# A gated recurrence, sixteen expert blocks and a gated FFN on one core: shorter lead in the first rounds, the first tokens as whole rows, gathers spread out, the last weights split earlier

## The chip, the core and the metric

The kernel runs as one program on one core of a Trainium2 chip. It uses the core's five engines: TensorE (PE), VectorE (DVE), ScalarE (ACT), GpSimd (POOL) and SyncE (SP, which here only starts transfers), and 16 DMA engines. The metric is the device time of one execution in microseconds (us). Three executions of the kernel before took 1109.24, 1110.06 and 1112.05 us; the median is 1110.06 us.

## The reference

Three steps follow one another, all in fp32. The first is a gated linear recurrence for 4 batches x 8 heads with a head size of 48, over 768 positions:

```
f = sigmoid(f_logit)
for t in range(768):
    state = f[t][:, None] * state + k[t] outer v[t]
    y[t]  = q[t] @ state
x = y.transpose(0, 2, 1, 3).reshape(3072, 384)
```

The second is a mixture of 8 experts (384 to 1024 to 384). Each of the 3072 tokens goes to the two experts with the largest noisy logits:

```
logits = x @ w_gate + log1p(exp(x @ w_noise)) * noise
w      = softmax of the two largest logits
out[token] = sum over its two experts e of  w_e * (relu(x[token] @ w1[e]) @ w2[e])
```

The third is `out = (silu(xn @ w_gate) * (xn @ w_val)) @ w_out` with `xn` the rms-normed tokens (times `rms_g`) and a middle size of 1536.

## The kernel before

**Fp32 products.** A large product is done as three products of operands that are split into a rounded high part and the rest (`three`, L650 to L656): high x high, high x low, low x high. A weight is split when a *part* of it is taken from its loaded tile (`Part.finish`, L192 to L209): an expert's part takes an ACT copy for `whi` (L208) and a DVE subtraction for `wlo` (L209). A part of the FFN comes as pairs of words of a 64-bit input, so it first goes through `narrow` (L177 to L181: one ACT and three DVE instructions for each of its 2 or 3 pieces), then the ACT copy (L204), and the subtraction runs on POOL (L205). Split parts lie in 18 slots, 8 of pool `wp` and 10 of pool `wp2`.

**Stage 1, the recurrence** (`gla_stream`). The sequence is cut into 24 chunks of 128 positions. Round i of the loop computes chunk i on PE: `scores` (L391), `keys` of the next chunk (four transposes, L172), `rows` of the previous chunk (the router's logits and the tokens, L453), `inter` (L431), `state` (L406) and `attend` (L441). What a chunk needs first is made in steps by ACT and DVE: `clip` (L327, L329), `gates` (L336, L337), `sums` (a scan, L343) and `prep` (exponentials L363 and L368, products KT L365 and QT L370). Round i runs `prep` for chunk i+2, `sums` for i+3, `gates` for i+4 and `clip` for i+5, so the first chunks of all of these must be ready before round 1 is through. `warm` puts filler matmuls (L1015) between the first rounds; there are 29. `columns` and `yT` are the operands of `rows`, `AM` the masked scores, `Ss` the running state.

**The router** (`router`) takes the logits of the first 1536 tokens, chooses their experts and makes lists of token numbers, `stoka` (L622). Its steps are put between the rounds by `plan`, a table of round numbers, at most three steps to a round (`safe`). One of its products, `bank<-r_both` (L514, L516), counts the tokens that go to each expert; it stands on PE behind `scores` of round 15.

**Gathers.** An expert block's tokens come by indirect transfers issued by POOL (L730): one instruction brings 128 pieces of 96 numbers (384 B), and a block of 384 tokens takes 12 of them. For the first block they stand in rounds 20 to 24 of `plan`, three to a round. Gathers of later blocks are given to units of the expert stage, two at most to a unit (`room`), except that those of block 1 pile up at unit 0, since there is no earlier unit: in the code that is `at_unit = max(at_unit, 0)`. `paced` makes a gather wait for the ACT instruction in `mark`, which is set by the expert stage. The gathered tokens `xg` are turned by a DVE transpose to `xt`, and split by ACT and DVE into `xhi` (L643) and `xlo` (L644). For block 0 this stands behind the recurrence.

**Stage 2, the experts and the FFN** (`expert_stream`). There are 128 units for the experts (16 blocks x 8 units: the first 8 blocks take early tokens from `stoka`, the other 8 the rest) and 72 for the FFN (6 blocks x 12). A unit is a first product (`l1`), an activation (`hhi` by ACT, `hlo` by DVE: L758 and L759 for experts, `sg`, L852 and L853 for the FFN) and a second product, two units later. After each unit `take_part` may split one part of the weights to come, in the order of the list `parts`. The FFN's 18 parts stand at the list's end; after one is taken, none is taken in the next two units (`count["rest"] = g_ + 2`).

PE follows the written order through both stages. In stage 1 so do ACT, DVE and POOL; in stage 2 a scheduler orders these.

Of the kernel before, what the change touches and what calls it, by code (L numbers as in the profile page):

```python
# [9 lines left out]
F32 = mybir.dt.float32  # L10
# [17 lines left out]
def tile_gated_attention_moe_ffn(  # L28
# [107 lines left out]
    stoka = cp.tile([P, 4, E, CAPA // P], I32, name="stoka")  # L136
    sel = ep.tile([P, 4, 4, 32], F16, name="sel")
# [126 lines left out]


# [47 lines left out]
    def load_v(n):  # L313
        b, c = divmod(n, NCH)
        nc.sync.dma_start(Vs[n % NV][:, :DM], v[b, c * P:(c + 1) * P])

# [58 lines left out]
    def keys(n):  # L375

        if n % NCH == NCH - 1:
            return
        p = cut(bank("K"), HP, P)
        for a in range(HP):  # L380
            flip(p[:, a, :], st["KT", n][:, a, :], ident)
        nc.scalar.activation(Ks[n % NK][:, :, :D],
                             p.rearrange("p a (b d) -> p (a b) d", b=2)[:, :, :D], AF.Copy)

    def scores(n):
        QT = st["QT", n]
        KT = st["KT", n]
        p = pa.tile([P, 2, HP, P], F32, name="scores")
        for h in range(H):
            o = 64 * (h % 2)  # L390
            nc.tensor.matmul(p[:, h % 2, h // 2, :], KT[o:o + D, h // 2, :],  # L391
                             QT[o:o + D, h // 2, :], start=True, stop=True)
        t = st["AM", n] = wk.tile([P, H, P], F32, name="AM", bufs=1)
# [41 lines left out]
    def attend(n):  # L435
        c = n % NCH
        pY = st["pY", n]
        for a in range(HP):
            for g in range(2):
                h = 2 * a + g  # L440
                nc.tensor.matmul(pY[64 * g:64 * (g + 1), a, :], Vs[n % NV][:, h * D:h * D + 64],  # L441
                                 st["AM", n][:, g * HP + a, :], start=not c and a == 0,
                                 stop=a == HP - 1, skip_group_check=True)
        y = wk.tile([P, HP, P], F32, name="yT", bufs=1)
        with tc.high_priority(30):
            nc.scalar.activation(y, pY, AF.Copy)
        st["yT", n] = y
# [57 lines left out]
    def router(n0, n1, rp):  # L505
# [59 lines left out]
        else:  # L565
# [3 lines left out]
                        float(-MIDDLE), op0=OP.min, op1=OP.max)  # L569
        yield  # L570
# [103 lines left out]
    late = {}  # L674
    mark = [None, None]
# [26 lines left out]
    def x_tiles(b, n):  # L702
        b.xhi = late["x"].tile([P, KD, 512], F32R, name="xhi")
        b.xlo = late["x"].tile([P, KD, 512], F32R, name="xlo")

    def h_tiles(n):
        return [xs_.tile([P, 512], F32R, name=nm, bufs=3) for nm in ("hhi", "hlo")]

    def moe_block(e, t0, N, pid):
# [12 lines left out]
        table = (xd[:NTA * P] if t0 == 0 else xd).rearrange("n (g d) -> (n g) d", g=4)  # L722

# [24 lines left out]
        b.turns = [lambda i=i: turn(i) for i in range(len(rows))]  # L748

# [19 lines left out]
        def post():  # L769
            for i, r in enumerate(rows):  # L770
                y = xs_.tile([P, DM], F32, name="y", bufs=3)
# [17 lines left out]
    def ffn_block(bi):  # L789
# [76 lines left out]
        def post(which=range(4)):  # L866
            for i in which:
                n = 4 * bi + i
                y = xs_.tile([P, DM], F32, name="y", bufs=3)
# [40 lines left out]
    free = [(wp, str(i), -1) for i in range(8)]  # L910
# [9 lines left out]
    def take_part(g_):  # L920
# [16 lines left out]
        if part.wide and units[g_][0] < NM:  # L937
            count["rest"] = g_ + 2
# [15 lines left out]


    wanted = []
    for i in range(1, len(blocks)):
# [63 lines left out]
    def gla_stream():  # L1021
# [3 lines left out]
        with tc.manual_schedule(engines=ALL):  # L1025
# [13 lines left out]
            nc.sync.dma_start(columns[:, :, NX:], moe_w_both[:, :, :2 * E])  # L1039
            for t in Vs:  # L1040
# [4 lines left out]
            run(prep, 0, PARTS)  # L1045
            warm(3)
            keys(0)
            next(rest)
            run(decay, 1)
            next(rest)  # L1050

            for i in range(NT + 2):
                routing.extend(plan.get(i, []))
                n = 4 + 2 * i if i < 2 else i + 6
                if (i < 2 or i % 2 == 0) and valid(n):
                    load_kq(n)
                if valid(i + 3):
                    load_v(i + 3)
                n = 6 + 2 * i if i < 2 else i + 8
                if (i < 2 or i % 2 == 0) and valid(n):  # L1060
                    load_f(n)
# [3 lines left out]
                if i == 0:  # L1065
                    warm(6)
                    run(prep, 1)
                more = prep(i + AHEAD) if i and valid(i + AHEAD) else iter(())
                next(more, None)
                if valid(i + 1):  # L1070
# [3 lines left out]
                if valid(i - 1):  # L1074
                    rows(i - 1)
                if valid(i):
                    inter(i)
                safe()
                next(more, None)
                if i == 0:  # L1080
                    warm(4)
                if valid(i):
                    state(i)
                    carry(i)
                    if i == 0:
                        attend(i)
                if i == 0:
                    warm(6)
                    run(decay, 2)
                    clip(3, scalar=False)  # L1090
                    gates(3)
                    run(prep, 2)
                    clip(4, scalar=False)
                if valid(i + 4):
                    gates(i + 4)
                if valid(i) and i:
# [30 lines left out]
    late["x"] = main.enter_context(tc.tile_pool(name="xl", bufs=2))  # L1127
    wp2 = main.enter_context(tc.tile_pool(name="wp2", bufs=1))
    late["cv"] = main.enter_context(tc.tile_pool(name="cv", bufs=2))
    free.extend((wp2, str(i), -1) for i in range(10))  # L1130
    for fn in blocks[0].turns:
        fn()
# [256 lines left out]
```

## Time and profile before

| | |
|---|---|
| Median of three executions | 1110.06 us |
| Profiled execution: its own time | 1109.45 us |
| Profiled execution: span | 1107.7 us |
| PE busy | 1049.3 us (95%) |
| DVE busy | 665.5 us (60%) |
| ACT busy | 484.6 us (44%) |
| POOL busy | 307.1 us (28%) |
| Recurrence: first `scores` to first expert matmul | 7.9 to 166.46 us |
| Experts: to first activation of the FFN | to 621.4 us |
| FFN: to the last matmul | to 1098.7 us |

The span runs from the first to the last instruction in the trace; the execution's own time holds 1.75 us more. In the rows below "PEclk" is the clock that PE was granted, as a share of 2.4 GHz. A time in square brackets at the end of a timeline row is how long the engine stood idle before it, and what it waited for; "issue" means that the profile shows nothing it waited for, "remote" that it waited for a semaphore whose setter the profile does not name.

### The profile page before, as it was taken

Reading aid. Unit: us, or ns where it says so; the run is one execution under the profiler, and the core shown is the slowest. Engines: PE = TensorE matmul, PEld = TensorE weight load, DVE = VectorE, ACT = ScalarE, POOL = GpSimd, SP = SyncE. Lnnn points to the kernel's source line nnn. Section 1 sums busy time; section 2 is a strip of 40 time slices with the busy share of each in tenths; the row PEclk is TensorE's granted clock in tenths of the full one; section 3 lists DMA queues with packets and bytes.
Section 4 is the critical chain, followed back from the end, with each engine's and each line's share of the span. In section 5 each row is a group of like instructions: output and inputs, shape, how many; then the busy total and the mean of one; then the engine's idle time right before and its main releaser. Section 6 shows DMA issues by size and latency. Waiting matters only on the chain.

```text
span 1107.7 us, 17452 instructions
## 1 busy us (share of the span) xinstructions
PE 1049.3 (95%) x6497; PEld 950.0 (86%) x6497; DVE 665.5 (60%) x1475; ACT 484.6 (44%) x1048; POOL 307.1 (28%) x327
## 2 busy tenths in 40 slices
PE   6998858999999999999999987899999999999996
PEld 4887748999999999899999976788888888888886
DVE  5889946977666656655555689545344454454332
ACT  5886624556555544454443545323223223232211
POOL 2000224544455544444441163220030020110000
PEclk8999977999999999999999998899999999999999
DMA  9976232667666655455443263020020110110000
GB/s 304 321 232 207 64 98 84 218 222 232 216 214 212 199 172 167 145 157 161 136 154 95 92 200 114 29 73 15 1 86 1 44 43 1 57 30 1 29 1 32
DMA packets 89138, 134.46 MB, mean 121 GB/s; under 512 B 8847, under 2 KB 65059, under 8 KB 89043
## 3 DMA queue, kind: packets, MB, share of 16 engines
q1 hardware_dynamic: 79475, 113.82, 31.3%
q0 software_dynamic: 9568, 19.43, 6.6%
q8 instruction: 53, 0.87, 0.3%
q14 instruction: 42, 0.34, 0.1%
HBM read 107.63 MB, written 25.59 MB: 120 GB/s over the span
## 4 chain that ended last, share of the span: by engine, by line
PE 76%; DVE 9%; issue 6%; DMA 4%; ACT 2%; POOL 1%; SPq 1%; POOLq 0%; DVEq 0%; ACTq 0%
PE bank L656 68%; DMA raw<-in_moe_w_dram 3%; PE bank L441 2%; PE scores L391 1%; PE bank L453 1%; PE bank L431 1%; PE bank L172 1%; DVE wlo L209 1%; PE bank L406 1%; DVE cv L179 1%; DVE AM L395 1%; DVE cv L181 1%; POOL wlo L205 1%; DVE cs L343 1%; DVE KT L365 1%
## 5 line engine op out<-in xcount | busy, mean ns | idle before, releaser
L656 PE MATMUL bank<-xhi,wlo 128*128 128x512 f32 (+8 forms) x816 | 305.0, 374 | 11.7 <-POOL wlo L205 10.6
L656 PE MATMUL bank<-xhi,whi 128*128 128x512 f32 (+8 forms) x816 | 305.7, 375 | 6.6 <-ACT xhi L643 4.7
L656 PE MATMUL bank<-xlo,whi 128*128 128x512 f32 (+8 forms) x816 | 304.0, 373 | 0.0
L656 PE MATMUL bank<-whi,hhi 128*128 128x384 f32 x728 | 245.6, 337 | 2.3 <-ACT y L775 0.9
L656 PE MATMUL bank<-whi,hlo 128*128 128x384 f32 x728 | 245.7, 337 | 0.9 <-issue 0.9
L656 PE MATMUL bank<-wlo,hhi 128*128 128x384 f32 x728 | 245.3, 337 | 0.4 <-issue 0.4
L656 PEld LDWEIGHTS bank<-xhi,wlo 128*128 128x128 f32 x816 | 155.5, 191 | 31.4 <-POOL wlo L205 11.9
L656 PEld LDWEIGHTS bank<-xhi,whi 128*128 128x128 f32 x816 | 155.4, 190 | 28.1 <-ACT xhi L643 4.9
L656 PEld LDWEIGHTS bank<-xlo,whi 128*128 128x128 f32 x816 | 155.3, 190 | 16.8 <-DVE xlo L644 0.3
L209 DVE TENSOR_TENSOR wlo<-raw,whi 128x256 fp32r<-128x256 f32 (+1 forms) x320 | 137.7, 468 | 31.9 <-ACT whi L208 26.3
L759 DVE SCALAR_TENSOR_TENSOR hlo<-bank,hhi 128x384 fp32r<-128x384 f32 (+7 forms) x128 | 73.2, 572 | 117.5 <-ACT hhi L758 106.9
L208 ACT ACTIVATE whi<-raw 128x256 fp32r<-128x256 f32 (+1 forms) x320 | 126.3, 451 | 32.2 <-DMA raw<-in_moe_w_dram 28.9
L656 PEld LDWEIGHTS bank<-whi,hhi 128*128 128x128 f32 x728 | 133.7, 184 | 7.6 <-DVE y L773 1.5
L656 PEld LDWEIGHTS bank<-wlo,hhi 128*128 128x128 f32 x728 | 133.3, 183 | 7.7 <-issue 1.0
L656 PEld LDWEIGHTS bank<-whi,hlo 128*128 128x128 f32 x728 | 133.3, 183 | 4.6 <-issue 1.2
L730 POOL DMA_INDIRECT xg<-xd,stokr x107 | 105.0, 981 | 106.3 <-ACT hhi L758 82.1
L730 POOL DMA_INDIRECT xg<-xd,stoka x96 | 100.4, 1045 | 112.7 <-ACT hhi L758 77.0
L758 ACT ACTIVATE hhi<-bank 128x384 fp32r<-128x384 f32 (+7 forms) x128 | 64.1, 501 | 152.2 <-PE bank L656 126.9
L849 DVE TENSOR_TENSOR sg<-bank,sg 128x512 f32<-128x512 f32 x72 | 49.7, 690 | 118.1 <-ACT sg L848 118.0
L800 POOL DMA_INDIRECT xg<-yd,slots x40 | 44.2, 1104 | 237.4 <-ACT hhi L852 207.4
L848 ACT ACTIVATE sg<-bank 128x512 f32<-128x512 f32 x72 | 42.9, 596 | 142.8 <-PE bank L656 136.3
L852 ACT ACTIVATE hhi<-sg 128x512 fp32r<-128x512 f32 x72 | 45.4, 630 | 116.9 <-DVE sg L850 116.7
(161 smaller groups left out, 1057.0 us busy)
## 6 DMA issues: line engine op xcount, KB each, us to landing
raw<-in_moe_w_dram SPq DMA_DIRECT2D x64, 768.0 KB
Qs<-in_kq_dram SPq DMA_DIRECT2D x11, 1024.0 KB
yd<-y SPq DMA_DIRECT2D x48, 192.0 KB
Fs<-in_f_logit_dram SPq DMA_DIRECT2D x11, 512.0 KB
Vs<-in_v_dram SPq DMA_DIRECT2D x24, 192.0 KB
xd<-x SPq DMA_DIRECT2D x24, 192.0 KB
ya<-y SPq DMA_DIRECT2D x24, 192.0 KB
raw<-in_moe_w_gate_dram SPq DMA_DIRECT2D x6, 768.0 KB
```

Of the source, the lines that this page charges most:

```text
L172: nc.tensor.transpose(p, x, i)
L208: nc.scalar.activation(hi[:, j], raw[:, j], AF.Copy)
L209: nc.vector.tensor_tensor(lo[:, j], raw[:, j], hi[:, j].bitcast(F32), op=OP.subtract)
L441: nc.tensor.matmul(pY[64 * g:64 * (g + 1), a, :], Vs[n % NV][:, h * D:h * D + 64], st["AM", n][:, g * HP + a, :], start=not c and a == 0, ...
L656: nc.tensor.matmul(o, a, b, start=start and i == 0, stop=stop and i == 2)
L730: paced(nc.gpsimd.indirect_dma_start(out=b.xg[i][:, k_], out_offset=None, in_=table, in_offset=bass.IndirectOffsetOnAxis(ap=rows_of[:, k_, ...
L758: mark[0] = nc.scalar.activation(hhi[:, :N], p[:, :N], AF.Relu).ins
L759: mark[1] = nc.vector.scalar_tensor_tensor(hlo[:, :N], p[:, :N], 0.0, hhi[:, :N].bitcast(F32), op0=OP.max, op1=OP.subtract).ins
L800: paced(nc.gpsimd.indirect_dma_start(out=y, out_offset=None, in_=ya if n < GROUP else yd, in_offset=bass.IndirectOffsetOnAxis(ap=at_, axis ...
L848: nc.scalar.activation(sg, ps[0], AF.Sigmoid)
L849: nc.vector.tensor_tensor(sg, ps[0], sg, op=OP.mult)
L852: mark[0] = nc.scalar.activation(hhi, sg, AF.Copy).ins
```

## The change

It has four parts.

1. In the first rounds each chunk is prepared one round later: round i does `prep` for i+1, `sums` for i+2, `gates` for i+3 and `clip` for i+4. In rounds 2, 3, 4 and 5 `clip`, `gates`, `sums` and `prep` in turn do two chunks (`due`), and from round 6 the lead is that of before. `keys` and `scores` are split from what follows them (`keys_out`, `masks`) in the prologue, `keys` stands behind `inter` while i is below 6, and 20 fillers are left of 29.
2. The first block's tokens come as 3 gathers of 128 whole rows (1536 B; `fetch_rows`) with the list `stok0`, in rounds 19 and 20. They are turned by 9 PE transposes in rounds 22 and 23 and split from PSUM (`turn_rows`). `xhi` and `xlo` move to the pool `xs_`, `hhi`, `hlo` and `y` to a late pool.
3. Eight of block 1's 12 gathers are issued in rounds 20 to 24, about two to a round, and paced by `yT`, which now sets `mark`. The router runs one step earlier.
4. Of the FFN's 18 loads of weights, 12 are put among the last 48 loads of the experts, one after every fourth. Slots are 6 of `wp` and 12 of `wp2`; the wait between the FFN's parts is one unit.

```diff
-    free = [(wp, str(i), -1) for i in range(8)]
+    EARLY = 24
+    experts = loads[:]
+    del loads[:], parts[:]
+    ...
+    ffn = loads[:]
+    loads[:] = experts[:-2 * EARLY]
+    for i, load in enumerate(experts[-2 * EARLY:]):
+        loads.append(load)
+        if i % 4 == 3 and wide:
+            loads.append(ffn.pop(0))
+    loads += ffn
+    parts[:] = [part for load in loads for part in load.parts]
+    free = [(wp, str(i), -1) for i in range(6)]
...
-            count["rest"] = g_ + 2
+            count["rest"] = g_ + 1
...
+        def fetch_rows(i):
+            b.xg[i] = xs_.tile([P, 4, DM // 4], F32, name="xg", bufs=6)
+            paced(nc.gpsimd.indirect_dma_start(
+                out=b.xg[i].rearrange("p b d -> p (b d)"), out_offset=None, in_=xd[:NTA * P],
+                in_offset=bass.IndirectOffsetOnAxis(ap=stok0[:, i:i + 1], axis=0)))
+        def turn_rows(i):
+            if i == 0:
+                x_tiles(b, N)
+            p = cut(bank("X"), KD, P)
+            x = b.xg[i].rearrange("p b (c k) -> p k (b c)", k=KD)
+            for j in range(KD):
+                flip(p[:, j], x[:, j], ident)
+            c = slice(i * P, (i + 1) * P)
+            split_x(b.xhi[:, :, c], b.xlo[:, :, c], p)
...
+        skip = GIVEN if i == 1 else 0
         for u, fns in zip(where, b.fetches):
+            fns, skip = fns[skip:], max(0, skip - len(fns))
...
+            def due(i, grows, lead):
+                if i < grows:
+                    ns = (i + lead,)
+                elif i == grows:
+                    ns = (i + lead, i + lead + 1)
+                else:
+                    ns = (i + lead + 1,)
+                return [n for n in ns if n < NT]
...
-                more = prep(i + AHEAD) if i and valid(i + AHEAD) else iter(())
+                short = i < 6
+                preps = due(i, 5, 1)
+                more = prep(preps[0]) if preps else iter(())
...
+                for n in preps[1:]:
+                    run(prep, n)
...
-                if valid(i + 4):
-                    gates(i + 4)
+                for n in due(i, 3, 3):
+                    gates(n)
+                    load_f_after(n)
...
-                if valid(i + 3):
-                    sums(i + 3)
-                if valid(i + 5):
-                    clip(i + 5)
+                for n in due(i, 4, 2):
+                    sums(n)
+                for n in due(i, 2, 4):
+                    clip(n)
...
-    plan = {12: [idle, step, step], 13: [idle, step], 14: [step, step], 15: [step], 16: [step],
-            17: [step], 18: [step], 19: [idle, step], 20: [step]}
-    for i, fn in enumerate([fn for fns in blocks[0].fetches for fn in fns]):
-        plan.setdefault(20 + (i + 1) // 3, []).append(fn)
+    plan = {12: [idle, step, step], 13: [idle, step, step], 14: [step, step], 15: [step],
+            16: [step], 17: [step], 18: [idle, step], 19: [step]}
+    plan[19] += [blocks[0].fetches[0][0], blocks[0].fetches[1][0]]
+    plan[20] = [blocks[0].fetches[2][0], idle]
+    then = [fn for fns in blocks[1].fetches for fn in fns][:GIVEN]
+    plan[20] += then[:1]
+    for k_ in range(3):
+        plan[21 + k_] = [then[1 + 2 * k_], idle, then[2 + 2 * k_]]
+    plan[24] = then[7:]
+    turning = {22: blocks[0].turns[:1], 23: blocks[0].turns[1:]}
...
-    for fn in blocks[0].turns:
-        fn()
+    free.extend((wp2, str(i), -1) for i in range(12))
```

Three places show how this moves instructions. The first is ACT at the start, before, from the gates of chunk 1 to the `yT` of chunk 0 and the gates behind it:

```order
L336 ACTIVATE L<-Fs_133 128x512
L337 ACTIVATE L<-L 128x512
L363 ACTIVATE Ek<-cs 128x512
L368 ACTIVATE cs<-cs 128x512
L382 ACTIVATE Ks_125<-bank_271 128x8x48
L446 ACTIVATE yT<-bank_277 128x512
L336 ACTIVATE L<-Fs_134 128x512
L337 ACTIVATE L<-L 128x512
L336 ACTIVATE L<-Fs_134 128x512
L337 ACTIVATE L<-L 128x512
L363 ACTIVATE Ek<-cs 128x512
L368 ACTIVATE cs<-cs 128x512
```

The same stretch now:

```order
L348 ACTIVATE L<-Fs_134 128x512
L349 ACTIVATE L<-L 128x512
L399 ACTIVATE Ks_125<-bank_215 128x8x48
L375 ACTIVATE Ek<-cs 128x512
L380 ACTIVATE cs<-cs 128x512
L348 ACTIVATE L<-Fs_135 128x512
L349 ACTIVATE L<-L 128x512
L469 ACTIVATE yT<-bank_267 128x512
L399 ACTIVATE Ks_126<-bank_280 128x8x48
L348 ACTIVATE L<-Fs_135 128x512
L349 ACTIVATE L<-L 128x512
L375 ACTIVATE Ek<-cs 128x512
```

Behind the first `yT` (L446, now L469) stood the gates of chunks 2 and 3 and the `prep` of chunk 2; the gates of chunk 2 now stand ahead of it, and those of chunk 3 behind it. The second place is PE around the router's product `r_both`, before:

```order
L431 MATMUL bank_1298<-QT,Ss_131 64x128 x8
L406 MATMUL bank_1322<-Vs_129,Ks_126 64x48 x8
L441 MATMUL bank_1298<-AM,Vs_129 64x128 x8
L391 MATMUL scores<-QT,KT 128x128 x8
L514 LDWEIGHTS before
L514 MATMUL bank_1364<-r_both,before 128x96
```

And now:

```order
L408 MATMUL scores<-QT,KT 128x128 x8
L173 MATMUL bank_1286<-ident,KT 128x128 x4
L476 MATMUL bank_1294<-columns,yT 128x112 x4
L454 MATMUL bank_1303<-QT,Ss_132 64x128 x8
L537 LDWEIGHTS before
L537 MATMUL bank_1312<-r_both,before 128x96
```

It stood behind `state`, `attend` and the next round's `scores` and stands ahead of them now. The third place is POOL from the recurrence on (`hs` is a small copy of each round), before:

```order
L372 COPY hs<-cs 128x4 x21
L730 DMA xg<-xd,stoka 128x96
L372 COPY hs<-cs 128x4
L730 DMA xg<-xd,stoka 128x96 x3
L372 COPY hs<-cs 128x4
L730 DMA xg<-xd,stoka 128x96 x92
```

And now:

```order
L384 COPY hs<-cs 128x4 x19
L750 DMA xg<-xd,stok_100 128x384
L384 COPY hs<-cs 128x4
L750 DMA xg<-xd,stok_100 128x384 x2
L384 COPY hs<-cs 128x4
L770 DMA xg<-xd,stoka 128x96 x2
L384 COPY hs<-cs 128x4
L770 DMA xg<-xd,stoka 128x96 x48
L206 TENSOR_TENSOR wlo_3359<-cv,whi_3358 128x768
L770 DMA xg<-xd,stoka 128x96 x12
L206 TENSOR_TENSOR wlo_3672<-cv,whi_3671 128x768
L770 DMA xg<-xd,stoka 128x96 x12
```

The FFN's subtractions on POOL (L205, now L206), which all stood behind the last expert gathers, now stand among them.

## Rows read from the trace of the kernel before

**Rows 1.** The page: the chain that ended last, its shares by engine.

```profile
PE 76%; DVE 9%; issue 6%; DMA 4%; ACT 2%; POOL 1%; SPq 1%; POOLq 0%; DVEq 0%; ACTq 0%
```

**Rows 2.** Windows: stretch, length, busy PE, PEld, DVE, ACT, POOL (x instructions), PEclk, DMA, GB/s.

```profile
40.00:50.00 10.00, 10.00 (x154) 8.82 (x154) 9.18 (x15) 8.51 (x16) 0.68 (x2) 1.00 1.02 338
300.00:400.00 100.00, 99.56 (x560) 97.29 (x559) 64.27 (x143) 54.06 (x135) 56.38 (x58) 1.00 0.65 209
621.40:718.10 96.70, 82.91 (x368) 70.21 (x368) 77.86 (x169) 47.35 (x105) 35.52 (x21) 0.91 0.35 112
718.10:794.10 76.00, 76.00 (x374) 67.05 (x373) 34.80 (x68) 21.77 (x38) 8.57 (x8) 1.00 0.11 32
```

**Rows 3.** Waits of PE, 500 to 800 us: us in total, times, longest.

```profile
PE bank L656 <- POOL wlo L205: 10.6, 3, 3.8
```

**Rows 4.** Groups by form, 560 to 740 us: busy, mean ns of one; idle before.

```profile
L205 POOL TENSOR_TENSOR wlo<-cv,whi 128x768 fp32r<-128x768 f32 x18 | 35.8, 1990 | 82.8 <-ACT whi L204 82.8
L181 DVE SCALAR_TENSOR_TENSOR cv<-raw,cv 128x256 int32<-128x256 int32 x36 | 16.9, 473 | 0.1
L179 DVE SCALAR_TENSOR_TENSOR cv<-raw,cv 128x256 int32<-128x256 int32 x36 | 14.7, 415 | 0.2
L178 DVE TENSOR_SCALAR cv<-cv 128x256 int32<-128x256 int32 x36 | 10.3, 295 | 1.1 <-ACT cv L177 1.1
```

**Rows 5.** DVE line L853, 620 to 712 us: ns min/median/max, first and last.

```profile
L853 DVE TENSOR_TENSOR hlo<-sg,hhi x11: 684/1156/2732, 624.9 to 707.8; 128x512 fp32r<-128x512 f32 x11
```

**Rows 6.** DVE line L853, 720 to 1090 us.

```profile
L853 DVE TENSOR_TENSOR hlo<-sg,hhi x59: 691/692/694, 721.5 to 1087.7; 128x512 fp32r<-128x512 f32 x59
```

**Rows 7.** Timeline of PE, first rounds: start, length, instruction, idle before.

```profile
19.73 1.16 PE L391 MATMUL scores<-QT,KT 48*128 48x128 f32 x16
...
30.68 1.87 PE L391 MATMUL scores<-QT,KT 48*128 48x128 f32 x16
```

**Rows 8.** Timeline of PE, round 15 and the start of 16.

```profile
98.47 0.20 PE L514 MATMUL bank<-r_both,before 128*128 128x96 bf16 x1 [1.56 <-DVE r_both L511]
...
101.48 0.67 PE L406 MATMUL bank<-Vs,Ks 128*64 128x48 f32 x16
...
103.00 1.16 PE L391 MATMUL scores<-QT,KT 48*128 48x128 f32 x16
```

**Rows 9.** Timeline of PE, `scores` of rounds 20, 21 and 23.

```profile
128.63 1.16 PE L391 MATMUL scores<-QT,KT 48*128 48x128 f32 x16
...
133.80 1.16 PE L391 MATMUL scores<-QT,KT 48*128 48x128 f32 x16
...
155.31 1.16 PE L391 MATMUL scores<-QT,KT 48*128 48x128 f32 x16
```

**Rows 10.** Timeline of POOL: first and last gather of block 0 and block 1.

```profile
132.51 1.30 POOL L730 DMA_INDIRECT xg<-xd,stoka  x1 [4.76 <-DVE stoka L622]
...
147.64 0.94 POOL L730 DMA_INDIRECT xg<-xd,stoka  x1 [0.30 <-issue]
170.78 0.95 POOL L730 DMA_INDIRECT xg<-xd,stoka  x1 [22.19 <-ACT hhi L758]
...
185.50 1.34 POOL L730 DMA_INDIRECT xg<-xd,stoka  x1 [0.30 <-issue]
```

**Rows 11.** Timeline of ACT, `yT` of chunk 21.

```profile
148.19 0.60 ACT L446 ACTIVATE yT<-bank 128x512 f32<-128x512 f32 x1 [10.55 <-remote]
```

**Rows 12.** Timeline of PE, first units of the expert stage.

```profile
166.46 0.69 PE L656 MATMUL bank<-xhi,whi 128*128 128x384 f32 x1 [4.72 <-ACT xhi L643]
...
172.26 0.33 PE L656 MATMUL bank<-xhi,wlo 128*128 128x384 f32 x1
...
182.83 0.33 PE L656 MATMUL bank<-xhi,whi 128*128 128x384 f32 x1
...
192.72 0.33 PE L656 MATMUL bank<-whi,hhi 128*128 128x384 f32 x1
```

**Rows 13.** The page, DMA queues: packets, MB, share of 16 engines.

```profile
q8 instruction: 53, 0.87, 0.3%
```

More of the change, by code (lines that the diff above doesn't have):

```diff
@@ L263, in expert_of @@
         return numbers[r]
+    late = {}
+    mark = [None, None]
     gla = ExitStack()
@@ L315, in load_v, with load_f_after, load_kq_after @@
         nc.sync.dma_start(Vs[n % NV][:, :DM], v[b, c * P:(c + 1) * P])
+    def load_f_after(n):
+        if n % 2 and n + 5 < NT:
+            load_f(n + 5)
+    def load_kq_after(n):
+        if n % 2 and n + 5 < NT:
+            load_kq(n + 5)
     def run(fn, n, cuts=WHOLE):
@@ L702, in x_tiles @@
     def x_tiles(b, n):
-        b.xhi = late["x"].tile([P, KD, 512], F32R, name="xhi")
-        b.xlo = late["x"].tile([P, KD, 512], F32R, name="xlo")
+        b.xhi = xs_.tile([P, KD, 512], F32R, name="xhi")
+        b.xlo = xs_.tile([P, KD, 512], F32R, name="xlo")
     def h_tiles(n):
-        return [xs_.tile([P, 512], F32R, name=nm, bufs=3) for nm in ("hhi", "hlo")]
+        return [late["h"].tile([P, 512], F32R, name=nm) for nm in ("hhi", "hlo")]
     def moe_block(e, t0, N, pid):
@@ L748, in moe_block @@
         b.turns = [lambda i=i: turn(i) for i in range(len(rows))]
+        if e == 0 and t0 == 0:
+            b.fetches = [[lambda i=i: fetch_rows(i)] for i in range(len(rows))]
+            b.turns = [lambda i=i: turn_rows(i) for i in range(len(rows))]
         def l1(f):
@@ L1044, in gla_stream @@
             run(decay, 0, PARTS)
-            run(prep, 0, PARTS)
-            warm(3)
-            keys(0)
-            next(rest)
-            run(decay, 1)
-            next(rest)
-            for i in range(NT + 2):
+            halves = [prep(0, s) for s in PARTS]
+            for _ in range(2):
+                for half in halves:
+                    next(half)
+            clip(1, scalar=False)
+            for _ in range(2):
+                for half in halves:
+                    next(half)
+            warm(3)
+            keys(0, copy=False)
+            gates(1)
+            keys_out(0)
+            scores(0, masked=False)
+            sums(1)
+            clip(2, scalar=False)
+            masks(0)
+            warm(2)
+            state(0)
+            more = prep(1)
+            next(more)
+            next(more)
+            next(rest)
+            next(more)
+            gates(2)
+            next(more)
+            carry(0)
+            warm(5)
+            inter(0)
+            attend(0)
+            sums(2)
+            keys(1)
+            clip(3, scalar=False)
+            gates(3)
+            clip(4, scalar=False)
+            next(rest)
+            load_f_after(1)
+            load_f_after(3)
+            load_kq_after(1)
+            def due(i, grows, lead):
[6 more added lines that the diff above has]
+                return [n for n in ns if n < NT]
+            for i in range(1, NT + 2):
                 routing.extend(plan.get(i, []))
-                n = 4 + 2 * i if i < 2 else i + 6
-                if (i < 2 or i % 2 == 0) and valid(n):
-                    load_kq(n)
                 if valid(i + 3):
                     load_v(i + 3)
-                n = 6 + 2 * i if i < 2 else i + 8
-                if (i < 2 or i % 2 == 0) and valid(n):
-                    load_f(n)
                 if valid(i):
@@ L1064, in gla_stream @@
                 safe()
-                if i == 0:
-                    warm(6)
-                    run(prep, 1)
-                more = prep(i + AHEAD) if i and valid(i + AHEAD) else iter(())
+                short = i < 6
+                preps = due(i, 5, 1)
+                more = prep(preps[0]) if preps else iter(())
                 next(more, None)
-                if valid(i + 1):
+                if valid(i + 1) and not short:
                     keys(i + 1)
@@ L1084, in gla_stream @@
                     carry(i)
[L1085 to L1093, printed above, removed]
-                if valid(i + 4):
-                    gates(i + 4)
-                if valid(i) and i:
+                for n in due(i, 3, 3):
+                    gates(n)
+                    load_f_after(n)
+                if valid(i):
                     attend(i)
-                if valid(i + 3):
-                    sums(i + 3)
-                if valid(i + 5):
-                    clip(i + 5)
+                for n in due(i, 4, 2):
+                    sums(n)
+                for n in due(i, 2, 4):
+                    clip(n)
                 safe()
```

40 lines of the change are left out of this document (28 added, 12 removed).

## Prediction

> **What bounds the kernel now.** I read the chain of waits first. It is PE for 76% [rows 1], so the end is set by PE almost everywhere, and a change counts where PE waits or runs at the lower of its two clocks. I then took windows of the stages. In the middle of the expert stage PE is busy for 99.56 of 100 us at full clock [rows 2]; nothing can be won there, and something can be lost. The first block of the FFN is another matter: it takes 96.70 us and the next one 76.00 us for about the same number of matmuls, with PE busy for 82.91 us and the mean granted clock at 0.91 [rows 2]. The table of PE's waits names POOL's subtraction `wlo` for 10.6 us of it [rows 3]. Last I followed PE's timeline through the start, the router and the passage from recurrence to experts, and found five places where the spacing of equal work breaks [rows 7 to 9, 12].
>
> In a full stretch of the recurrence, 40 to 50 us, DVE is busy for 9.18 and ACT for 8.51 us of 10 [rows 2]. So the recurrence is held by these two as much as by PE, and what an early round leaves undone has to fit in there.
>
> **The change, part by part.** The sum is made against the profiled execution (1109.45 us), which lies 0.6 us below the median of 1110.06; I make no correction for that.
>
> *FFN weights early.* One FFN part costs DVE 3 x (0.295 + 0.415 + 0.473) = 3.55 us in three pieces, and POOL 1.99 us for `wlo` [rows 4]. DVE's busy time in the first FFN block is 77.86 us against 34.80 in the second [rows 2]; the 43.1 us between are 12 parts. They come when PE is about to use them, and PE stops. Twelve of 18 parts move into the expert stage, about one in 8 units, and by the order of taking the last six are then split some 8 units ahead of their use. The block can shrink by 96.70 - 76.00 = 20.7 us. The smallest gain, if only PE's idle time goes and the lower clock stays, is 96.70 - 82.91 = 13.8. I take **-20**, near the first end, because idle time and lower clock have one cause here: the second block, with the same matmuls and no splits, has neither.
> What is added: 12 x 3.55 = 42.6 us on DVE and 12 x 1.99 = 23.9 us on POOL, beside the experts' own parts. A unit takes (621.4 - 166.46) / 128 = 3.55 us, and the 12 parts spread over some 95 units, 337 us. DVE goes from 0.64 [rows 2] to 0.64 + 42.6 / 337 = 0.77, POOL from 0.56 to 0.63. That cover hides them; without it they cost up to 66 us (third rival). The experts' own lead falls with the slots they lose, from about 15 units to 3 at the least, 10 us, still more than the 3.55 + 1.99 of one part in between.
> A rule speaks against this. The trace has DVE's `hlo` at 0.69 us in the FFN's later blocks [rows 6], and at a median of 1.156 and up to 2.732 us in the first block, where POOL subtracts [rows 5]. The Trainium skill, page "SBUF — State Buffer", section "Who interferes with whom", says why such a pair may meet: a DVE instruction with both inputs in SBUF and a GpSimd instruction that reads SBUF exclude each other for the whole instruction. The trace agrees with it. By that rule the 12 moved subtractions take up to 12 x (2.73 - 0.69) = 24.5 us more out of DVE in the expert stage; an estimate from the rows, which would put DVE at 0.84 there, still hidden by the mean but less safely.
>
> *The gathers of the recurrence.* `scores` of rounds 20 and 21 are 5.17 us apart; from round 21 to 23 it takes 21.51 us [rows 9], 11.2 more than two rounds. In that time POOL issues 12 gathers, 132.51 to 147.64 us, nearly back to back [rows 10], and ACT's `yT` starts 10.55 us late on a semaphore that no row names, just as the last gather is issued [rows 11]. The change issues 11 gathers in place of 12 over rounds 19 to 24, and each waits for a `yT`, so they come about two to a round, 2.8 us of POOL (15.13 us / 11 steps = 1.38 each) in 5.2. Bounds: 0 and -11.2. I take **-9**: the delay hangs on the dense run, but 11 gathers remain. Behind the gathers that now wait stand the last three `hs` copies of POOL; `prep` runs two rounds ahead there, so each has about 10 us before it is used.
>
> *The second run of gathers.* POOL issues block 1's 12 gathers from 170.78 to 185.50 us [rows 10]. PE's matmuls of 384 columns are 0.173 us apart before (61 steps in 10.57 us), and at 182.83 us the 21 steps to 192.72 take 9.89 us instead of 3.64 [rows 12]: 6.25 lost. Eight of the 12 are issued earlier now. Bounds 0 and -6.3; I take **-6**.
>
> *First block's tokens.* PE waits 4.72 us for `xhi` before the first expert matmul at 166.46, and then runs 17 steps in 5.80 us, 0.341 each, at half clock, instead of 17 x 0.173 = 2.95 [rows 12]. Both go if PE turns the tokens in rounds 22 and 23: -4.7 - 2.85. The 9 transposes stand in PE's order: at the step of a 384-column matmul 9 x 0.173 = 1.6, at half that clock 3.1; nothing shorter than free is possible, so the bounds are -7.6 and, if the wait merely moves, +1.6. I take **-6**, since gathers issued in rounds 19 and 20 have two rounds to land.
>
> *First rounds.* `scores` of rounds 1 and 2 are 10.95 us apart [rows 7], 5.8 more than the 5.17 of round 20. Of the gates and the `prep` that stood between, one chunk's worth goes. It must be given back in rounds 2 to 5, where ACT and DVE have 0.8 to 1.5 us free in 10 [rows 2]: up to one round, 5.17. Bounds: -5.8 (given back for nothing) and +5.2 (wait stays, work is added). I take **-3**, in the middle of the range's better half, because the late start comes from work that is not needed yet.
>
> *Router.* PE waits 1.56 us for `r_both` and the product stands behind `state`, `attend` and `scores` [rows 8]. Now it stands ahead of them: 103.00 + 1.16 - 101.48 = 2.68 us of PE's work sooner. If DVE is no sooner, PE waits 4.24 us, 2.7 more. One step of the router is also moved up, which helps, and a wait of 4 us may be followed by half clock (2.85 as above). Bounds 0 and +5.6; I take **+3**.
>
> Sum: -20 - 9 - 6 - 6 - 3 + 3 = -41, and 1109.45 - 41 = **1068 us**. All best ends: -20.7 - 11.2 - 6.3 - 7.6 - 5.8 = -51.6, 1058. The likeliest case's own range is 1057 to 1077.
>
> **Rivals.**
>
> *1. The two dense stalls do not hang on how dense the gathers are.* For it: in 300 to 400 us POOL is busy for 56 us with 58 instructions, mostly gathers, and PE loses 0.4 us [rows 2]; so gathers alone do not stop PE. Against it: the two stalls end as the two runs end [rows 10 to 12]. Then -9 and -6 fall away: 1068 + 15 = 1083.
> Such a stall could be late instructions. The page's queue q8 brought 0.87 MB in 53 packets, 16.4 KB each [rows 13]. The Trainium skill, page "Runtime: NRT & Kernel Launch", section "Instruction fetch mechanics", says that an engine refills its instructions in 16 KiB blocks by a DMA queue of its own while it goes on, mostly hidden; the packet size agrees, but no row shows an engine without instructions. By that the stalls would return wherever the next block is due, and the sum is this rival's.
>
> *2. The last six FFN parts still hold PE.* For it: six parts remain to be split beside the start of the FFN, 21 us of DVE. Against it: they are taken some 8 units ahead. Then only the idle part or less comes, -13.8 at the lower clock: 1074; with rival 1 as well, 1089.
>
> *3. Slower: the early parts stand in PE's way.* If the FFN's splitting on DVE and POOL is served ahead of the `hlo` and `wlo` that PE needs next, each of the 12 parts costs 3.55 + 1.99 = 5.54 us of PE, 66 us in all: 1068 + 66 = 1134. Place: the second half of the experts. It turns slower than before from 41 / 12 = 3.4 us lost per part. For it: the long `hlo` [rows 5]. Against it: DVE is free for 36 us in 100 [rows 2], and `hlo` is used two units, 7 us, after its `l1`. The rule of the SBUF page named above is the mechanism that would bring it about.
>
> **How the numbers follow.** Forecast 0.62, rival 1 0.18, rival 2 0.14, rival 3 0.06. The range of 1056 to 1086 holds the forecast nearly whole, most of rival 2 and a good part of rival 1, about 8 in 10. A difference under 0.3% (3.3 us) is not told from none. Faster 0.93: the first three cases, less 0.01 for a first round and a router at their worst ends on top of rivals 1 and 2. The third rival and that 0.01 make same 0.02 (losses of about 3.4 us per part) and slower 0.05.
>
> **What would show it.** FFN first block: the stretch from the first `sg` to the next block's at 76 to 79 us, no wait of PE for `wlo`, and clock 1.00. Wrong if over 83 us. Gathers: `scores` of rounds 21 to 23 spaced by 5 to 6 us, no gap named "remote" on ACT, no half clock there. Tokens: no wait for `xhi`, the first expert matmul at full clock about 20 us earlier than 166.46. Start: round 2 about 3 to 6 us earlier, rounds 3 to 6 a little longer. Router: a wait of 3 to 4 us before `r_both`. Experts: PE busy over 99% in the middle still, and a wait for `wlo` or `hlo` there, summing to more than a few us, would show the third rival. The forecast as a whole is wrong if the FFN block keeps more than half of its excess.

## The result, and the profile after

The changed kernel took 1068.88 us (median of four, 1065.75 to 1070.27) against 1109.65 of the kernel before on the same chip: 0.964 of its time, 95% interval 0.959 to 0.969. The forecast was 1068. The profiled execution took 1068.86 us, 40.6 less than the one of before.

The chain that ended last, by engine; it answers to [rows 1]:

```profile
PE 83%; DVE 7%; ACT 3%; DMA 3%; issue 2%; SPq 1%; another core or an unknown queue 1%; DVEq 0%; ACTq 0%
```

Windows of the first two FFN blocks (columns as in [rows 2]):

```profile
601.98:677.01 75.03, 75.03 (x368) 66.01 (x367) 54.44 (x106) 30.87 (x63) 17.62 (x13) 1.00 0.21 67
677.01:753.02 76.01, 76.01 (x374) 67.03 (x373) 34.78 (x68) 21.75 (x38) 8.90 (x8) 1.00 0.11 32
```

The first block no longer differs from the second: no idle time, clock 1.00. PE's waits of the whole span (us, times, longest):

```profile
PE bank L476 <- ACT yT L469: 5.9, 5, 2.0
PE bank L537 <- DVE r_both L534: 3.9, 1, 3.9
...
PE bank L681 <- ACT xhi L668: 2.7, 1, 2.7
PE bank L681 <- DVE hlo L802: 2.2, 3, 1.3
```

The 10.6 us for `wlo` [rows 3] are gone, and so is the wait for `xhi` of the first block; the 2.7 us here belong to a later one, and together with `hlo` they are new. PE's timeline at the places of [rows 7 to 9, 12]:

```profile
14.14 1.16 PE L408 MATMUL scores<-QT,KT 48*128 48x128 f32 x16
...
21.18 1.16 PE L408 MATMUL scores<-QT,KT 48*128 48x128 f32 x16
...
93.63 0.24 PE L537 MATMUL bank<-r_both,before 128*128 128x96 bf16 x1 [3.94 <-DVE r_both L534]
...
95.23 1.94 PE L464 MATMUL bank<-AM,Vs 128*64 128x128 f32 x16
...
102.77 1.16 PE L408 MATMUL scores<-QT,KT 48*128 48x128 f32 x16
...
125.83 1.16 PE L408 MATMUL scores<-QT,KT 48*128 48x128 f32 x16
130.90 1.16 PE L408 MATMUL scores<-QT,KT 48*128 48x128 f32 x16
...
141.00 1.16 PE L408 MATMUL scores<-QT,KT 48*128 48x128 f32 x16
...
149.36 0.42 PE L681 MATMUL bank<-xhi,whi 128*128 128x384 f32 x1
...
152.42 0.33 PE L681 MATMUL bank<-xhi,wlo 128*128 128x384 f32 x1
```

Rounds 21 to 23 are 5.05 us apart. The wait for `r_both` has grown from 1.56 to 3.94 us, and `attend` behind it, 1.94 us in place of 1.1, shows half clock. The same events in both traces give the lead at each place:

| Event | before | after | lead | step |
|---|---|---|---|---|
| `scores`, round 13 | 83.40 | 79.31 | 4.09 | start -4.1 |
| `scores`, round 16 | 103.00 | 102.77 | 0.23 | router +3.9 |
| `scores`, round 20 | 128.63 | 125.83 | 2.80 | made up -2.6 |
| `scores`, round 23 | 155.31 | 141.00 | 14.31 | gathers -11.5 |
| 18th expert matmul | 172.26 | 152.42 | 19.84 | tokens -5.5 |
| `hhi` of unit 8 | 199.73 | 173.66 | 26.07 | second run -6.2 |
| first `sg` of the FFN | 621.42 | 601.98 | 19.44 | experts +6.6 |
| first `sg` of its second block | 718.11 | 677.01 | 41.10 | FFN -21.7 |

### The profile page after: what moved, and what is told of

Its sections match the earlier page's. It is cut to its first block, busy times and chain, and to the rows that moved or that the text cites. A ratio compares the mean times of both kernels' runs of the same rounds, so it can differ in the third digit from the quotient of the medians.

```text
span 1067.0 us, 17429 instructions
## 1 busy us (share of the span) xinstructions
PE 1029.9 (97%) x6497; PEld 935.8 (88%) x6497; DVE 669.1 (63%) x1473; ACT 482.5 (45%) x1048; POOL 300.0 (28%) x318
## 4 chain that ended last, share of the span: by engine, by line
PE 83%; DVE 7%; ACT 3%; DMA 3%; issue 2%; SPq 1%; another core or an unknown queue 1%; DVEq 0%; ACTq 0%
PE bank L681 76%; DMA raw<-in_moe_w_dram 2%; PE bank L173 1%; PE bank L476 1%; PE bank L454 1%; PE bank L464 1%; PE scores L408 1%; DVE cs L355 1%; DVE wlo L210 1%; DVE AM L418 1%; DMA columns<-in_moe_w_both_dram 1%; PE bank L429 1%; DVE xt L781 0%; DVE hlo L802 0%
## 5 line engine op out<-in xcount | busy, mean ns | idle before, releaser
L681 PE MATMUL bank<-xhi,wlo 128*128 128x512 f32 (+8 forms) x816 | 301.1, 369 | 0.0
L681 PEld LDWEIGHTS bank<-xhi,wlo 128*128 128x128 f32 x816 | 153.2, 188 | 18.5
L210 DVE TENSOR_TENSOR wlo<-raw,whi 128x256 fp32r<-128x256 f32 (+1 forms) x320 | 142.3, 482 | 22.8 <-ACT whi L209 13.0
L770 POOL DMA_INDIRECT xg<-xd,stokr x107 | 107.5, 1004 | 95.4 <-ACT hhi L801 71.3
L770 POOL DMA_INDIRECT xg<-xd,stoka x84 | 89.3, 1063 | 91.0 <-ACT hhi L801 57.8
```

What stands on the lines that cost most here:

```text
L210: nc.vector.tensor_tensor(lo[:, j], raw[:, j], hi[:, j].bitcast(F32), op=OP.subtract)
L681: nc.tensor.matmul(o, a, b, start=start and i == 0, stop=stop and i == 2)
L770: paced(nc.gpsimd.indirect_dma_start(out=b.xg[i][:, k_], out_offset=None, in_=table, in_offset=bass.IndirectOffsetOnAxis(ap=rows_of[:, k_, ...
```

## The experiments

They ran on three chips, four kernels on each, which share the runs of the kernel before. It took 1112.56 us on the first, 1113.02 on the second and 1098.28 on the third, so times are compared on one chip only, and effects of one place by events in the traces. "Drift" is how far a kernel falls behind the changed kernel's first trace from unit 22 to unit 118 (`hhi`); kernels with the same expert stage had 2.3 and 2.8 on the first chip, 0.5 to 3.3 on the second (0.9 for the changed kernel itself, the control), -3.4 and -3.8 on the third. The kernel before had -6.8.

**FFN weights late again.**

```diff
-    loads[:] = experts[:-2 * EARLY]
-    ...
+    loads[:] = experts + ffn
...
-            count["rest"] = g_ + 1
+            count["rest"] = g_ + 2
```

> The changed kernel with its fourth part undone: the FFN's loads stand at the end of the list again and two units are left free between its parts; the slots stay 6 and 12. In the trace after, the FFN's first block is 21.7 us shorter than before (75.0 against 96.7), and the expert stage from its 9th to its last unit is 6.5 us longer. Theory: both come from the early parts, the loss because DVE's narrowing stands ahead of hlo and xhi. Then this kernel has a first FFN block of about 96 us, no PE waits for hlo or xhi of over 1 us between units 34 and 66, and takes 1069 + 21.7 - 6.5 = 1084 us. Rival: the 6.5 us come from other slots and pools; then the expert stage stays as in the changed kernel and the time is about 1090 us.

It took 1092.81 us. The first FFN block takes 95.99 us (600.10 to 696.09), and the drift is -5.5, some 8 less than its neighbours' 2.3 and 2.8. PE's waits:

```profile
PE bank L681 <- POOL wlo L206: 10.8, 3, 3.8
```

A neighbour with the early parts took 1079.43 (the one with `r_both` put back, below): 13.4 less, in line with 21 won in the block less 8 lost among the experts. No wait of PE for `hlo` or `xhi` between units 34 and 66 is over 0.7 us now. The theory holds as to both. The absolute time missed by 9 us; the kernel before takes only 3 us more on this chip than beside the first runs of the changed kernel, the neighbour 10 us more than those.

**Gathers not paced.**

```diff
-            mark[0] = mark[1] = nc.scalar.activation(y, pY, AF.Copy).ins
+            nc.scalar.activation(y, pY, AF.Copy)
```

> The changed kernel without the pacing of gathers by yT in the recurrence: the same 11 gathers in the same order, but each may go as soon as the list of tokens is there. Theory (the stall hangs on how dense the gathers run): POOL issues eight to ten of them nearly back to back from round 20 on, the spacing of scores over two of rounds 20 to 23 grows from 10 to about 15 to 20 us, ACT's yT waits for a semaphore that no row names, and the time is 1074 to 1080 us. Rival (the stall does not hang on density but falls where engines fetch instructions, or hung on the 12 small gathers of block 0): no gap over 1 us, 1068 to 1070 us.

1086.24 us, 6.8 over the same neighbour. Eight gathers run from 135.54 to 146.19 us. PE and ACT in that time:

```profile
141.19 1.16 PE L408 MATMUL scores<-QT,KT 48*128 48x128 f32 x16
144.79 2.05 PE L476 MATMUL bank<-columns,yT 128*128 128x112 f32 x8 [2.44 <-issue]
...
150.87 1.16 PE L408 MATMUL scores<-QT,KT 48*128 48x128 f32 x16
```

```profile
144.14 0.60 ACT L469 ACTIVATE yT<-bank 128x512 f32<-128x512 f32 x1 [4.34 <-remote]
```

A round takes 9.7 us in place of 5.05, with the same unnamed wait of ACT as in [rows 11], and half clock behind it. The theory holds for the place; the total lies 6 us over its range, as totals on this chip lie over theirs wherever the start is the changed one.

**The kernel before, paced.** The same line put into the kernel before.

> The kernel before with nothing but the pacing: each gather of the recurrence waits for the newest yT, up to three to a round. Theory of density: no stall from round 21 to 23, scores about 5.2 us apart there, 8 to 11 us won at that place; the last gathers come later, so the wait for xhi in front of the first expert matmul may grow by some us; 1099 to 1106 us. Rival: the stall stays near 11 us wherever the gathers stand, 1108 to 1112 us.

1106.48 us, ratio 0.995 (0.993 to 0.997). The first expert matmul comes at 158.45 us, 8.0 sooner than in [rows 12], though the wait for `xhi` is 5.29. From round 21 to 23 it takes 12.5 us, not 21.5. Block 1's 12 gathers still stand close (162.77 to 177.12), and PE still stops there:

```profile
175.15 0.33 PE L657 MATMUL bank<-xlo,whi 128*128 128x384 f32 x1 [0.24 <-issue]
176.58 0.33 PE L657 MATMUL bank<-xhi,wlo 128*128 128x384 f32 x1 [1.10 <-issue]
178.00 0.67 PE L657 MATMUL bank<-whi,hhi 128*128 128x384 f32 x1 [1.09 <-issue]
```

One run spaced out, its stall shrinks; the other left dense, its stall stays. The total lies 0.5 us outside the range that the theory gave, 1.5 us better than the rival's.

**The router's product put back.**

```diff
-14: [step, step], 15: [step],
+14: [step], 15: [step, step],
```

> The changed kernel with the router's product r_both back behind scores of round 15, all other router steps where they are. In the trace after, PE waits 3.94 us for it, followed by 3.6 us at the lower clock (1.6 us lost). Theory: the wait falls to about 1.3 us and the lower clock goes, since state, attend and scores (2.7 us) are done in the meantime; scores of round 16 start 3 to 4 us sooner, of which the rounds behind, held by DVE, keep 1 to 3: 1066 to 1068 us. Rival: DVE's chain behind r_both sets the gathers and the end of the recurrence, and comes no sooner: 1068 to 1070 us.

The wait is gone, and round 16 starts 20.62 us behind round 13, not 23.46. But another wait for DVE has come:

```profile
PE bank L454 <- DVE Ss L443: 2.5, 1, 2.5
```

From round 13 to 23 it is 61.71 us against 61.69. The rival was right: PE's place for this product is worth nothing. The 1079.43 us lie some 10 us over both ranges; the changed kernel itself takes about as long on another chip (next).

**The changed kernel again.**

> The changed kernel once more, unaltered, as the measure for the others on the same chip. In two of the kernels that share its first rounds, the product r_both put back and the gathers not paced, PE fell to half clock at 17.3 to 24 us and 38.4 to 45 us, behind waits of 1.73 us (columns) and 1.91 us (yT); in the first profile of the changed kernel it did not. Theory: the first rounds stand at the edge, and the changed kernel falls too in some executions: 1068 to 1076 us. Rival: the fall belongs to those other kernels: 1066 to 1070 us, clock 1.00 from 10 to 50 us.

1078.69 us (1070.27 to 1080.90), ratio 0.969 (0.966 to 0.973). In this trace the clock falls in the first rounds, where the first trace had 1.00:

```profile
10.00:20.00 10.00, 10.00 (x89) 6.46 (x85) 8.08 (x14) 5.99 (x12) 2.74 (x18) 0.71 1.11 342
...
30.00:40.00 10.00, 7.96 (x100) 6.66 (x98) 6.11 (x10) 6.72 (x12) 0.38 (x2) 0.82 1.02 340
40.00:50.00 10.00, 9.24 (x106) 7.74 (x102) 7.47 (x11) 6.70 (x12) 0.90 (x2) 0.84 0.94 329
```

The time is 3 us over the range I gave, but the theory holds: the change left a start that keeps its clock in some executions only. One of the six here took 1070.27 us at a mean clock of 0.994, the others 1076 to 1081 at 0.985 to 0.988. The start is only part of the difference, though: of the 7.3 us between the two profiled executions, 2.6 are there at round 13, and 2.7 come between units 8 and 22 at full clock, without a cause that a run shows.

**The start of before.** `gla_stream`'s prologue and rounds are those of the kernel before, with the turning of the tokens kept.

> The changed kernel with the prologue and the rounds of the kernel before (prep two chunks ahead at once, 29 fillers, keys ahead of inter); gathers, turning, router steps and weights as changed. In the trace after, scores of round 2 start at 21.18 against 30.68 us, those of round 6 at 45.46 against 50.8, those of round 13 at 79.31 against 83.4 us. Theory: the shorter lead is worth the 4.1 us that are left at round 13: 3 to 5 us slower than the changed kernel of the same chip where its clock holds. Rival: DVE and ACT make up the late start by round 20, and nothing or 1 us is lost.

1077.21 us beside 1078.69. Round 13 starts at 81.55 us, in the control at 81.93. Here the shorter lead is worth nothing: the clock falls in the control, and in this kernel too (0.83 from 10 to 30 us). Where it held from 20 us on, in the first trace and in the next kernel, round 13 starts at 79.31 and 79.59 us, 2.0 to 2.2 us sooner than here. The 3 to 5 us are not shown.

**Fillers at the waits.**

```diff
+                if i in (1, 4, 5):
+                    warm(6)
                 if valid(i - 1):
                     rows(i - 1)
```

> The changed kernel with six filler matmuls (about 1.4 us) in front of the router's product of the previous chunk in rounds 1, 4 and 5, where PE waits 1.7 to 2.0 us. Theory: PE's clock holds in the first rounds in every execution, scores of round 6 start by 46 us and those of round 13 by 80 us, and the kernel is at or below the fastest of the changed kernel's executions, 3 to 6 us under executions whose clock fell. Rival: the clock falls elsewhere in the first rounds, or the fillers hold PE up: no gain, or 1 to 2 us lost.

1074.88 us (1070.20 to 1076.91). Round 13 starts at 79.59 us, and the clock is 1.00 from 20 to 50 us, 0.88 from 10 to 20. The median is 3.8 under the control, but the intervals of the ratios overlap (0.964 to 0.970 and 0.966 to 0.973), and not every execution reached the fastest of the control. Likely a gain; not shown.

**Early parts in the second half.**

```diff
-    EARLY = 24
+    EARLY = 12
...
-        if i % 4 == 3 and wide:
+        if i % 2 == 1 and wide:
```

> The changed kernel with the same 12 early loads of the FFN put among the last 24 loads of the experts, one after every second, not the last 48: their parts are then split at units 69 to 124 rather than 29 to 124; the last six stay where they are. In the trace after the expert stage loses 8.4 us between units 34 and 66, where four of the parts fall and PE waits for hlo and xhi, and nothing from unit 66 on. Theory: a unit of the first blocks (3.1 us) has no room for 3.55 us of narrowing, a later one (4.0 us) has: 5 to 8 us faster than the changed kernel of the same chip, the first FFN block stays at 75 us. Rival: the loss goes with the parts, now more dense; no gain, and waits for hlo and xhi between units 69 and 124.

1070.07 us against the control's 1078.69; ratios 0.962 (0.959 to 0.965) and 0.969 (0.966 to 0.973). The drift is -7.5 against 0.9. The same stretch, the control and then this kernel:

```profile
250.00:370.00 120.00, 114.26 (x644) 111.34 (x643) 88.69 (x199) 67.80 (x174) 72.52 (x67) 1.00 0.68 214
```

```profile
250.00:370.00 120.00, 119.44 (x677) 117.18 (x676) 81.06 (x182) 66.97 (x170) 63.84 (x65) 1.00 0.68 213
```

The first FFN block takes 75.0 us as before. What the theory forecast holds: in the second half the same parts cost nothing. That the longer unit is the reason is not shown; with `wlo` on DVE (the last experiment) they cost little in the short units too.

**Both edits together.**

> The two edits that helped, together: the early FFN loads among the last 24 expert loads, and six fillers in rounds 1, 4 and 5. Alone they gave 1070.07 us (ratio to before 0.9616) and 1074.88 us (0.9665) where the changed kernel took 1078.69 (0.9691). Theory: they act at different places and add, 1078.69 - 8.6 - 3.8 = 1066 us, ratio about 0.957 to 0.960. Rival: the first rounds fall to half clock anyway, and nothing is added to the one: 1069 to 1071 us, ratio 0.961.

1063.80 us (1061.79 to 1067.20), the lowest of all, and 5.9 us or more under the three others on its chip. But the kernel before took 1098.28 there, so the ratio is 0.969 and misses the expected one. The changed kernel did not run on that chip; that this version beats it rests on the drift (-8.3, neighbours -3.4 and -3.8) and on round 13 at 79.41 us with clock 1.00. In the nine traces of the changed start without these fillers, round 13 starts between 79.3 and 84.9 us, and in eight of them the clock falls somewhere between 10 and 50 us; in the two with the fillers it starts at 79.4 and 79.6.

**Turned behind the recurrence.**

```diff
-    turning = {22: blocks[0].turns[:1], 23: blocks[0].turns[1:]}
+    turning = {}
     gla_stream()
+    for fn in blocks[0].turns:
+        fn()
```

> The changed kernel with the first block's tokens still fetched as whole rows in rounds 19 and 20, but turned by PE behind the last round, not in rounds 22 and 23. Theory: PE then waits about 3 to 5 us for xhi and xlo in front of the first expert matmul (three turns, each with its split behind it), less the 2.4 us that turning takes in rounds 22 and 23 now, and may fall to half clock behind the wait, 2.9 us: 1 to 6 us slower than the changed kernel on the same chip. Rival: the wait before came from the late gathers alone, and turning late costs nothing: within 1 us.

1074.20 us, and 1073.51 for the next kernel; the changed kernel did not run on this chip. Round 13 starts at 81.02 us, in the next kernel at 81.07, so the two can be compared up to the first units: `hhi` of unit 0 comes at 157.21 and 152.99 us. Turning late costs 4.2 us, as expected, in waits of PE for the splits:

```profile
150.37 0.61 PE L173 MATMUL bank<-ident,xg 128*128 128x128 f32 x3 [1.21 <-DVE xlo L669]
152.16 0.91 PE L173 MATMUL bank<-ident,xg 128*128 128x128 f32 x3 [1.17 <-DVE xlo L669]
153.65 0.69 PE L681 MATMUL bank<-xhi,whi 128*128 128x384 f32 x1 [0.58 <-ACT xhi L668]
```

**Block 1's gathers dense.**

```diff
-    GIVEN = 8
+    GIVEN = 0
...
-    plan[20] += then[:1]
-    ...
-    plan[24] = then[7:]
```

> The changed kernel without the eight gathers of block 1 in the recurrence: all 12 stand at the first units of the expert stage, as before. The three row gathers stay. Theory: rounds 20 to 23 stay 5.1 us apart, and PE stalls near the end of the 12 dense gathers again, 5 to 8 us between units 3 and 6, with half clock behind it: 6 us slower than the changed kernel on the same chip. Rival: the stall before had to do with the state of that run; no stall, within 1 us.

1073.51 us. From unit 3 to unit 8 it loses 6.8 us to the changed kernel's first trace, as expected. But the way is another:

```profile
175.32 0.69 DVE L781 STREAM_TRANSPOSE xt<-xg 128x384 f32<-128x384 f32 x1 [5.19 <-DMA xg<-xd,stoka]
```

```profile
178.85 0.63 PE L681 MATMUL bank<-xhi,whi 128*128 128x384 f32 x1 [5.08 <-DVE hlo L802]
```

The last gather, issued at 169.72, lands late; DVE waits for it with `hlo` behind, and PE waits for `hlo`. So 12 dense gathers cost 6.8 us at this place, by a wait that has a name here and had none before.

**`wlo` of the FFN's parts on DVE.**

```diff
-                nc.gpsimd.tensor_tensor(lo, t, hi.bitcast(F32), op=OP.subtract)
+                nc.vector.tensor_tensor(lo, t, hi.bitcast(F32), op=OP.subtract)
```

> The changed kernel with wlo of the FFN's parts taken on DVE, not on POOL; nothing else. In the trace after, DVE's wlo of the experts takes up to 2.11 us while POOL subtracts, 0.42 us else, and hlo starts late behind 2.4 to 3.6 us of narrowing. Theory: the time that DVE spends in order ahead of hlo is what PE waits for; about 0.8 to 1.3 us more of it for each of 12 early parts, waits for hlo and xhi grow, 2 to 8 us slower than the changed kernel on the same chip. Rival: DVE and POOL keep each other from their operands, and that is the larger cost; the expert stage gets 2 to 6 us shorter.

1069.73 us; the drift is -7.1, 3.5 better than its neighbours with the same early parts. In the changed kernel (ns min/median/max, first and last start):

```profile
L206 POOL TENSOR_TENSOR wlo<-cv,whi x13: 1842/1849/1864, 250.1 to 599.8; 128x768 fp32r<-128x768 f32 x13
...
L210 DVE TENSOR_TENSOR wlo<-raw,whi x262: 371/422/2111, 200.1 to 586.0; 128x256 fp32r<-128x256 f32 x78, 128x384 fp32r<-128x384 f32 x53
```

With the subtraction on DVE:

```profile
L206 DVE TENSOR_TENSOR wlo<-cv,whi x12: 912/950/959, 257.1 to 593.3; 128x768 fp32r<-128x768 f32 x12
...
L210 DVE TENSOR_TENSOR wlo<-raw,whi x272: 373/422/596, 199.7 to 586.8; 128x256 fp32r<-128x256 f32 x81, 128x384 fp32r<-128x384 f32 x55
```

My theory fell and the rival holds: DVE does the subtraction in half of POOL's time, its other work no longer stretches to 2.11 us, and PE's waits for `hlo` among the experts fall to 0.3 us, from 2.0 and 1.6 in its neighbours:

```profile
PE bank L681 <- DVE hlo L802: 0.3, 1, 0.3
```

This is the rule of the Trainium skill, page "SBUF — State Buffer", section "Who interferes with whom": a DVE instruction with two SBUF inputs and a GpSimd one that reads SBUF exclude each other. The trace agrees. The narrowing still stands ahead of `hlo`, and the subtraction now too:

```profile
303.38 0.62 DVE L179 TENSOR_SCALAR cv<-cv 128x384 int32<-128x384 int32 x2
303.92 1.02 DVE L180 SCALAR_TENSOR_TENSOR cv<-raw,cv 128x384 int32<-128x384 int32 x2
304.86 1.02 DVE L182 SCALAR_TENSOR_TENSOR cv<-raw,cv 128x384 int32<-128x384 int32 x2
305.79 0.56 DVE L802 SCALAR_TENSOR_TENSOR hlo<-bank,hhi 128x384 fp32r<-128x384 f32 x1
306.47 0.96 DVE L206 TENSOR_TENSOR wlo<-cv,whi 128x768 fp32r<-128x768 f32 x1
307.35 0.55 DVE L802 SCALAR_TENSOR_TENSOR hlo<-bank,hhi 128x384 fp32r<-128x384 f32 x1
```

The parts stand at the same units as in the neighbours, and yet the drift is only 1.2 short of the -8.3 that the kernel with parts in the second half has on this chip. POOL, freed of the subtraction, can also issue its gathers sooner; what that gives was not told apart.

## Why the prediction was right

The total was right to 1 us, and most of its steps too.

*FFN weights, -20.* Measured -21.7, a microsecond beyond the bound, for the reason given. What failed is the step "That cover hides them": the sum had nothing for the expert stage, and it lost 6.6 us. The mean load of DVE hid the moment. `hlo` stands in order behind one part's narrowing:

```profile
298.93 1.02 DVE L180 SCALAR_TENSOR_TENSOR cv<-raw,cv 128x384 int32<-128x384 int32 x2
299.87 1.02 DVE L182 SCALAR_TENSOR_TENSOR cv<-raw,cv 128x384 int32<-128x384 int32 x2
300.81 0.55 DVE L802 SCALAR_TENSOR_TENSOR hlo<-bank,hhi 128x384 fp32r<-128x384 f32 x1
```

PE waits 1.32 us for it at 301.41. This is the third rival at a tenth of its price, and between units 34 and 66, not in the second half of the experts. But the place in line is the smaller part: with `wlo` on DVE the narrowing stands in front of `hlo` all the same, and PE hardly waits. On that chip moving `wlo` recovered 3.5 us and moving the parts 4.7 (drift -7.1 and -8.3 against -3.6). So there some three quarters of the loss went with POOL's subtraction, for which I had worked out up to 24.5 us and then called them hidden "by the mean". On the second chip moving the parts recovered 8.4; `wlo` on DVE was not run there.

*Gathers of the recurrence, -9.* Measured -11.5, the whole excess. Both experiments on pacing bear the step out. The first rival fell for this run. Its queue brings the same 53 packets in the kernels with the stall and without it; when they came, no row shows.

*Second run, -6.* Measured -6.2. Dense again, the loss is back in size; its mechanism is not one and the same in the two kernels.

*Tokens, -6.* Measured -5.5; the turning in the rounds alone is worth 4.2.

*Start, -3, and router, +3.* At round 13 the start had -4.1, and by round 16 the router had taken 3.9 of it, with half clock behind its wait. The rounds to 20 gave back 2.6. Together the two came to -2.8, where the sum had 0. The router's term was no cost of PE's order, since undoing it gains nothing. The start's term is real only where the clock holds, which I had not weighed: I counted 29 fillers down to 20 as nothing. The profiled execution was lucky here: its 79.31 us is the lowest of the nine traces, whose middle one has 81.93, only 1.5 us before the 83.40 of the kernel before.

The errors, -2.8 at the start, -2.5 and -1.7 at gathers and FFN and +6.6 at the experts, cancel. The hit on the total is luckier than the single terms.

Left open: where the time between units 8 and 22 goes on the second chip; what the parts in the second half and `wlo` on DVE would give together, which was not run; why dense gathers make PE and ACT wait with no named releaser in two places, while ten gathers in a row (172.99 to 189.4 us in the changed kernel) do not; and why the kernel before is 1.3% faster on one chip, where the ratio was not measured for the changed kernel.

## What to carry to other kernels

Work that is moved under cover must be set against what runs beside it at that moment, not against an engine's mean load: on one chip twelve early parts spread over units 29 to 124 cost 4.7 us with their subtraction on POOL and 1.2 us with it on DVE, both against the same parts in the second half. Spread indirect transfers by a dependency on steady work, one or two to a round. A start with waits of 1.7 to 2 us on PE may keep its clock in one execution and lose it in the next, so a control on the same chip belongs to each comparison of a few microseconds.

## What the hardware showed that I had not expected

The 128x768 subtraction takes 1.85 us on POOL and 0.95 us on DVE, and while POOL does it, a DVE subtraction of 0.42 us takes up to 2.11. The kernel before took 1098.3 to 1113.0 us on different chips, and the changed one 1068.9 and 1078.7, the slower one with granted clocks of 0.71 to 0.84 in its first rounds where the faster one had 1.00.
